# Top-k attention with an ELU feed-forward block: prologue and weight decoding in a written order at two pace levels, exponential and gate for pairs of groups

## The chip, the core and the metric

The kernel runs on one core of a Trainium2 chip. Its engines work side by side, each through a queue of its own: TensorE (PE, matrix products and transposes), VectorE (DVE), ScalarE (ACT), GpSimd (POOL) and SyncE (SP, which here only issues transfers). They wait for each other through semaphores. The metric is the time of one execution in microseconds (us), as the median of several runs.

## The reference

Eight batches of eight heads, 576 tokens, head size 64, all in 32-bit floats. For each row of scores the 32 largest are kept, the others are masked away, and the softmax runs over what is left. The heads of one token are laid side by side (512 numbers), and a feed-forward block follows with an ELU between its products. The two weights come as 64-bit floats.

```python
scores = scale * np.matmul(q, k.transpose(0, 1, 3, 2))
kth = np.partition(scores, -top_k, axis=-1)[..., -top_k:-top_k + 1]
scores = np.where(scores >= kth, scores, -1000000000.0)
attn = np.exp(scores - np.max(scores, axis=-1, keepdims=True))
attn = attn / (np.sum(attn, axis=-1, keepdims=True) + 1e-09)
x = np.matmul(attn, v)          # (B,H,S,D) -> (B*S, H*D)
h = x @ w_in                    # 4608 x 512 by 512 x 2048
g = np.where(h > 0.0, h, np.exp(np.minimum(h, 0.0)) - 1.0)
return g @ w_out                # 2048 x 512
```

## The kernel before

**Attention in steps.** A step is one tile of 128 query rows for one pair of heads; there are 144 of them. For each step PE makes the scores of both heads into PSUM (`scores`, line 291), ScalarE scales them into SBUF (line 308), and VectorE finds the 32nd largest of each row by four maxima of eight and three replacements (lines 319 to 329 in the first eight steps, 341 to 353 later): 14 operations of about 0.74 us. `mask` (lines 366 to 370, GpSimd and ScalarE) turns the row into exponentials, `normalise` (lines 380 to 387, GpSimd) divides, `turn` (line 406) transposes on PE with copies on ScalarE (407), and `attend` (line 432) multiplies by v. Scores are made two steps ahead of the selection; the mask, the transposes and the product with v follow one to three steps behind it.

**Feed-forward in blocks and pieces.** 128, 256 or 384 tokens (a block of one, two or three slots) go through the feed-forward part together, once all their heads are attended (`finish`). Blocks 0 to 4 have one slot, the other fourteen two or three. A block has 16 pieces `hidden(f)`, one for each group of 128 of the 2048 hidden columns, and four pieces `project(s, part)` for each slot. `hidden` makes a product into one of two PSUM buffers (line 490), and three ScalarE operations: n = Relu(-h) (line 502), g = Relu(h) (503), n = exp(-n) (504). VectorE then closes the gate: g + n - 1 (line 471), which is the ELU. A gate isn't issued at once. It goes into the list `gates` with the place at which it was made, and `close_gates(2)` issues it two places later; `project` closes all that are pending, and `hidden` closes the oldest if more than three are. n has five buffers (four for block 0).

**The order of the work.** A planner written in Python issues the pieces between the attention's instructions. Each step has four places, `feed(n, 0.25)`; at each, `feed` works out from the blocks' due times and the pieces' costs (`HIDDEN`, `PROJECT`) how much feed-forward work to issue. From step 8 (`tight`) on the engines take their instructions in just the order in which they are issued (`manual_schedule`). In the steps before it, and in the prologue before those (lines 616 to 633), a scheduler picks by readiness, at compile time.

**The weights' decoding.** The weights are decoded on the chip in 32 pieces of 128 x 512. SP loads one (`load_weight`, 512 KB) into one of three raw buffers; `convert_first` works on its words with three ScalarE operations (lines 169 to 171) and a GpSimd clamp (172), `convert_last` with two VectorE operations (179, 182) and a GpSimd addition into the weight (186). `hook`, called twice in each row's selection in the first eight steps (four times a step) and three times a step later, issues one `decode_piece(i)`: load piece i+2, first half of piece i, last half of piece i-1. A feed-forward piece isn't issued before the weights that it needs are decoded (`decoded`); blocks after the first need all of them. When the last piece is issued, the raw buffers' space goes to the later pools (`late`).

**The prologue** loads k and q of two head pairs and two pieces of weights on SP's queue, transposes k and q (`transpose_qk`, lines 258 to 276), makes the scores of steps 0 and 1, and loads the rest of the first batch.

Of the kernel before, what the change touches and what calls it, by code (L numbers as in the profile page):

```python
# [80 lines left out]
def kernel(  # L81
# [34 lines left out]
    wkpool = pool("wk", 1)  # L116
    etpool = pool("et", 2)
    small = pool("small", 4)
    xtpool = pool("xt", 2)
    opool = pool("o", 1)  # L120
    ps_sc = pool("ps_sc", 1, space=PSUM)
    ps_t = pool("ps_t", 2, space=PSUM)
# [2 lines left out]
    late = {}  # L125
    raws = ExitStack()
    early = raws.enter_context(tc.tile_pool(name="early", bufs=1))
    earlyf = raws.enter_context(tc.tile_pool(name="earlyf", bufs=4))
    rawpool = raws.enter_context(tc.tile_pool(name="raw", bufs=3))

    ident = const.tile([P, P], FP32, tag="ident", name="ident")
    make_identity(nc, ident[:])
# [15 lines left out]
        return moe_w_out[f * P : (f + 1) * P, :], w_out[:, f, :]  # L148

    def load_weight(i):  # L150
        t = rawpool.tile([P, 4 * WN], U32, tag="raw", name="raw")
        nc.sync.dma_start(t[:, 0 : 2 * WN], weight(i)[0])
        raw[i] = t

    def parts(t):
        words = t[:, 0 : 2 * WN].rearrange("p (n w) -> p n w", w=2)
        return words[:, :, 0], words[:, :, 1], t[:, 2 * WN : 3 * WN], t[:, 3 * WN :]

    def convert_first(i):

        lo, hi, e, m = parts(raw[i])
        ef, mf = e.bitcast(FP32), m.bitcast(FP32)
        nc.scalar.activation(ef, hi.bitcast(FP32), AF.Abs, scale=2.0**-48)
        nc.scalar.activation(mf, lo, AF.Copy, scale=2.0**-29, bias=2.0**23)  # L170
        nc.scalar.activation(m.bitcast(I32), mf, AF.Copy, bias=-(2.0**23))
        nc.gpsimd.tensor_scalar(
            ef, ef, (2.0 - 2.0**-3 - 2.0**-23) * 2.0**-32, 2.0**-63, ALU.min, ALU.max
        )

    def convert_last(i):
        t, dst = raw.pop(i), weight(i)[1]
        lo, hi, e, m = parts(t)
        nc.vector.tensor_scalar(
            e, e, 0x0FFFFFFF, 3, ALU.bitwise_and, ALU.logical_shift_left  # L180
        )
        nc.vector.scalar_tensor_tensor(
            out=e, in0=hi, scalar=0x80000000, in1=e,
            op0=ALU.bitwise_and, op1=ALU.bitwise_or,
        )
        nc.gpsimd.tensor_tensor(
            dst.bitcast(I32), e.bitcast(I32), m.bitcast(I32), ALU.add
        )

    decode = []  # L190
# [2 lines left out]
    def hook():  # L193

        if not decode:
            return
        decode.pop(0)()
        if not decode:
            raws.close()
            late["f"] = ctx.enter_context(tc.tile_pool(name="f", bufs=5))  # L200
            late["g"] = ctx.enter_context(tc.tile_pool(name="g", bufs=2))
            late["x"] = ctx.enter_context(tc.tile_pool(name="x", bufs=2))

    def decode_piece(i):
        if i < 2 * NF:
            if i + 2 < 2 * NF:
                load_weight(i + 2)
            convert_first(i)
        if i > 0:
            convert_last(i - 1)  # L210
            decoded[0] = i

    loaded, kqT, vT = {}, {}, {}

    def load_qk(b, hp):

        for name, src in (("k", k), ("q", q)):
            n = J + 1 if name == "k" else J
            t = ldpool.tile([P, n, 2, D], FP32, tag=name + "in", name=name + "in")
            if name == "k":  # L220
                last = t
            for hh in range(2):
                nc.sync.dma_start(
                    t[:, 0:J, hh, :],
                    src[b, 2 * hp + hh, 0:JP, :].rearrange("(p j) d -> p j d", j=J),
                )
            nc.sync.dma_start(
                last[0:R, J, :, :] if name == "k" else last[R:P, J, :, :],
                src[b, 2 * hp : 2 * hp + 2, JP:S, :].rearrange("h p d -> p h d"),
            )  # L230
            loaded[b, hp, name] = t
# [81 lines left out]
    def select_row(u, i):  # L313
        if i == 0:
            u.first = small.tile([P, 2, 8], FP32, tag="m1", name="m1")
            u.last = small.tile([P, 2, 8], FP32, tag="m4", name="m4")
        sc = u.sc[:, i, :]
        m = u.first[:, i, :]
        nc.vector.max(m, sc)
        wk = wkpool.tile([P, S], FP32, tag=f"wk{i}", name="wk")  # L320
        cur = sc
        for r in range(TOP_K // 8 - 1):
            nc.vector.match_replace(wk[:], m, cur, TAKEN)  # L323
            cur = wk[:]
            if r < TOP_K // 8 - 2:
                m = small.tile([P, 8], FP32, tag=f"m{i}", name="m")[:]
            else:
                m = u.last[:, i, :]
            nc.vector.max(m, cur)  # L329
            if r != 1:  # L330
                hook()
                yield

    def select(u):
# [117 lines left out]

    def finish(blk, parts, at, cols, src):
        if blk.xT is None:
            if blk.slots == 1 and late:
                blk.xT = late["x"].tile([P, NC, P], FP32, tag="xT", name="xT")
            else:
                blk.xT = xtpool.tile([P, NC, T], FP32, tag="xT", name="xT")
        nc.scalar.copy(blk.xT[:, at, cols], src)
        blk.left -= parts  # L460
        if blk.left == 0:
            ffn.extend(ffn_pieces(blk))
# [1 line left out]
    gates = []  # L464
    place = [0]

    def close_gates(keep=0):

        while gates and gates[0][0] <= place[0] - keep:
            _, dst, n = gates.pop(0)  # L470
            nc.vector.scalar_tensor_tensor(  # L471
                out=dst, in0=n, scalar=-1.0, in1=dst, op0=ALU.add, op1=ALU.add
            )

    def ffn_pieces(blk):
        n_tok = blk.slots * P

        def hidden(f):
            if f == 0 and blk.number == 0:
                g = early.tile([P, NF, P], FP32, tag="g", name="gT")  # L480
                blk.gT = [g[:, 0:NG], g[:, NG:NF]]
            elif f % NG == 0 and blk.number > 0:
                g = late["g"].tile([P, NG, T], FP32, tag="g", name="gT")
                blk.gT.append(g[:])
            if len(gates) > 3:
                gates[0] = (-1, *gates[0][1:])
                close_gates(place[0])
            ps = ps_f.tile([P, dm], FP32, tag="f", name="hps")
            for i in range(NC):
                nc.tensor.matmul(  # L490
                    ps[:, 0:n_tok],
                    w_in[:, i, f * P : (f + 1) * P],
                    blk.xT[:, i, 0:n_tok],
                    start=(i == 0),
                    stop=(i == NC - 1),
                )
            if blk.number == 0:
                n = earlyf.tile([P, P], FP32, tag="n", name="n")[:]
            else:
                n = late["f"].tile([P, T], FP32, tag="n", name="n")[:, 0:n_tok]  # L500
            g = blk.gT[f // NG][:, f % NG, 0:n_tok]
            nc.scalar.activation(n, ps[:, 0:n_tok], AF.Relu, scale=-1.0)  # L502
            nc.scalar.activation(g, ps[:, 0:n_tok], AF.Relu)  # L503
            nc.scalar.activation(n, n, AF.Exp, scale=-1.0)  # L504
            gates.append((place[0], g, n))

        def project(s, part):
            close_gates()
            if part == 0:
                blk.o = ps_f.tile([P, dm], FP32, tag="f", name="ops")  # L510
            step = NF // 4
            for f in range(part * step, (part + 1) * step):
                nc.tensor.matmul(  # L513
                    blk.o[:],
                    blk.gT[f // NG][:, f % NG, s * P : (s + 1) * P],
                    w_out[:, f, :],
                    start=(f == 0),
                    stop=(f == NF - 1),
                )
# [93 lines left out]
            fed["sum"] += cost  # L613
            piece()

    load_qk(0, 0)
    for i in range(2):
        load_weight(i)
    load_qk(0, 1)
    load_v(0, 0)  # L620
    start_qk(0, 0)
    turn_qk(True)
    scores(steps[0])
    load_qk(0, 2)
    start_qk(0, 1)
    turn_qk(True)
    scores(steps[1])
    load_qk(0, 3)
    for hp in range(1, NHP):
        load_v(0, hp)  # L630
    decode += [lambda i=i: decode_piece(i) for i in range(2 * NF + 1)]
    at(0, start_qk, 0, 2)
    at(1, start_qk, 0, 3)

# [5 lines left out]
    for n in range(NS + 3):  # L640
# [20 lines left out]
                feed(n, 0.25)  # L661
            continue
        if n == tight:
            E = mybir.EngineType
            ctx.enter_context(
                tc.manual_schedule(engines={E.PE, E.Activation, E.DVE, E.Pool})
            )
        passes = select(cur) if cur else iter(range(4))
        if ahead:
            scores(ahead)  # L670
# [59 lines left out]
```

## Time and profile before

| | |
|---|---|
| median of three runs | 1694.66 us (1693.64 to 1695.99) |
| the profiled execution | 1695.23 us, of which the profile's span is 1693.4 us |
| TensorE (PE) | 1597.5 us busy, 94% |
| VectorE (DVE) | 1542.7 us, 91% |
| ScalarE (ACT) | 1179.6 us, 70% |
| GpSimd (POOL) | 627.0 us, 37% |
| granted TensorE clock | 0.974 of full speed in the mean; 0.60 from 40 to 80 us, 0.59 from 80 to 120 us, 1.00 from 160 us on |

The span runs from the first instruction to the last. A row of tenths cuts it into 40 equal slices of 42.3 us, where each digit is an engine's busy share (9 is 90% or more). A line such as "L353 DVE" is the work of line 353 of the kernel on that engine. In a list of waits the name behind the arrow is what ended the wait. An engine that is busy all the time in a stretch sets the time of that stretch; idle time of another costs nothing there.

### The profile page before, as it was taken

The numbers are of one execution on the slowest core, as the hardware profiler recorded it, in microseconds if no ns is written. First come the engines' busy times: TensorE is split into PE (matmuls) and PEld (weight loads), VectorE is DVE, ScalarE is ACT, GpSimd is POOL, SyncE is SP. The second block draws the span as 40 slices with busy tenths as digits, with TensorE's granted clock in tenths as the row PEclk, the third lists the DMA queues.
The fourth block names the chain that finished last, engine by engine and source line by source line (L and its number), as shares of the span: only waits on it lengthen the run. The fifth ranks groups of instructions, "written<-read, shape, count | busy, mean of one in ns | idle before, by whom it ended". The sixth has DMA issues, their size and how long they took to land.

```text
span 1693.4 us, 26805 instructions
## 1 busy us (share of the span) xinstructions
PE 1597.5 (94%) x8560; PEld 1035.0 (61%) x8560; DVE 1542.7 (91%) x3248; ACT 1179.6 (70%) x2813; POOL 627.0 (37%) x1719
## 2 busy tenths in 40 slices
PE   4568899999999999999999999999999999999999
PEld 3355676667575666756557575755557575755565
DVE  6889999999999999999999999999998999998600
ACT  5787776778776776857758585867758686857531
POOL 3675333343333333433333333333333333332200
PEclk8568999999999999999999999999999999999999
DMA  5531021001200111001100111001100000000000
GB/s 156 169 130 63 15 56 36 7 1 42 51 12 7 29 35 42 1 14 42 43 19 1 28 42 35 7 10 46 36 20 8 21 21 28 7 7 7 7 13 13
DMA packets 101131, 56.25 MB, mean 33 GB/s; under 512 B 84096, under 2 KB 92288, under 8 KB 100992
## 3 DMA queue, kind: packets, MB, share of 16 engines
q1 hardware_dynamic: 100992, 54.55, 11.7%
q8 instruction: 68, 1.11, 0.3%
q14 instruction: 71, 0.58, 0.1%
HBM read 45.09 MB, written 9.44 MB: 32 GB/s over the span
## 4 chain that ended last, share of the span: by engine, by line
PE 68%; DVE 21%; ACT 5%; issue 2%; POOL 2%; DMA 1%; SPq 0%; ACTq 0%; POOLq 0%; DVEq 0%
PE ops L513 25%; PE hps L490 21%; PE avps L432 8%; DVE wk L346 7%; PE scps L300 7%; DVE m L353 6%; PE eps L406 5%; DVE m L341 2%; DVE gT L471 1%; DVE wk L323 1%; DVE m L329 1%; PE qkps L270 1%; ACT sc L370 1%; ACT sc L369 1%; ACT et L407 1%
## 5 line engine op out<-in xcount | busy, mean ns | idle before, releaser
L353 DVE MAX8 m<-wk 128x8 f32<-128x576 f32 x816 | 574.9, 745 | 0.0
L490 PE MATMUL hps<-xT,w_in 128*128 128x256 f32 (+2 forms) x2432 | 554.3, 376 | 19.3 <-ACT gT L503 19.3
L513 PE MATMUL ops<-w_out,gT 128*128 128x512 f32 x1152 | 522.6, 598 | 0.0
L490 PEld LDWEIGHTS hps<-xT,w_in 128*128 128x128 f32 x2432 | 409.5, 194 | 119.9 <-ACT gT L503 26.4
L346 DVE MATCH_REPLACE8 wk<-m,wk 128x576 f32<-128x576 f32 x544 | 399.4, 741 | 0.0
L513 PEld LDWEIGHTS ops<-w_out,gT 128*128 128x128 f32 x1152 | 208.4, 190 | 232.8 <-issue 201.0
L380 POOL TENSOR_SCALAR dene<-den 128x2 f32<-128x2 f32 x144 | 34.9, 243 | 819.6 <-ACT sc L370 819.0
L369 ACT ACTIVATE sc<-sc,neg 128x576 f32<-128x576 f32 x288 | 226.5, 787 | 56.6 <-POOL neg L366 56.1
L370 ACT ACTIVATE sc<-sc,gap 128x576 f32<-128x576 f32 x288 | 223.2, 775 | 26.6 <-ACT sc L369 1.9
L308 ACT ACTIVATE sc<-scps 128x576 f32<-128x576 f32 x288 | 173.4, 661 | 82.4 <-PE scps L300 82.4
L387 POOL TENSOR_SCALAR sc<-sc,rec 128x576 f32<-128x576 f32 x288 | 218.7, 769 | 15.2 <-POOL rec L385 0.4
L300 PE MATMUL scps<-kqT 64*128 64x288 f32 (+1 forms) x1280 | 198.1, 438 | 21.5 <-ACT sc L308 14.7
L471 DVE SCALAR_TENSOR_TENSOR gT<-n,gT 128x256 f32<-128x256 f32 (+2 forms) x304 | 129.1, 431 | 95.3 <-ACT n L504 95.3
L407 ACT COPY et<-eps 128x512 f32<-128x512 f32 x288 | 167.4, 581 | 61.8 <-PE eps L406 61.8
L406 PEld LDWEIGHTS eps<-ident,sc 128*128 128x128 f32 x1152 | 144.5, 145 | 93.4 <-issue 48.9
L346 DVE MATCH_REPLACE8 wk<-m,sc 128x576 f32<-128x576 f32 x272 | 199.7, 741 | 0.0
L432 PE MATMUL avps<-et,vT 128*64 128x256 f32 (+2 forms) x2080 | 191.0, 325 | 9.0 <-ACT et L407 8.4
L406 PE MATMUL eps<-ident,sc 128*128 128x128 f32 x1152 | 177.9, 280 | 21.8 <-POOL sc L387 18.6
L341 DVE MAX8 m<-sc 128x8 f32<-128x576 f32 x272 | 191.3, 744 | 0.0
L432 PEld LDWEIGHTS avps<-et,vT 128*64 128x64 f32 x2080 | 122.3, 140 | 80.4 <-issue 24.7
L502 ACT ACTIVATE n<-hps 128x256 f32<-128x256 f32 (+2 forms) x304 | 112.6, 370 | 84.2 <-PE hps L490 79.0
L300 PEld LDWEIGHTS scps<-kqT 64*128 64x128 f32 (+1 forms) x1280 | 106.0, 180 | 90.2 <-issue 45.1
(47 smaller groups left out, 1236.6 us busy)
## 6 DMA issues: line engine op xcount, KB each, us to landing
kin<-in_k_dram SPq DMA_DIRECT2D x64, 128.0 KB, 2.8
qin<-in_q_dram SPq DMA_DIRECT2D x64, 128.0 KB, 2.8
raw<-in_moe_w_in_dram SPq DMA_DIRECT2D x16, 512.0 KB, 3.9
vT<-in_v_dram SPq DMA_DIRECT2D x64, 128.0 KB, 2.3
raw<-in_moe_w_out_dram SPq DMA_DIRECT2D x16, 512.0 KB, 3.3
out_dram<-osb SPq DMA_DIRECT2D x32, 256.0 KB, 2.2
kin<-in_k_dram SPq DMA_DIRECT2D x32, 32.0 KB, 2.5
kin<-in_q_dram SPq DMA_DIRECT2D x32, 32.0 KB, 2.2
```

The source lines that it names most:

```text
L300: nc.tensor.matmul(wide[i][rows, half, 0:HS], kq[part, q0 : q0 + u.t.ql], kq[part, k0 : k0 + HS], start=True, stop=True,)
L341: nc.vector.max(found[i], cur[i])
L346: nc.vector.match_replace(wk[i], found[i], cur[i], TAKEN)
L353: nc.vector.max(found[i], cur[i])
L369: nc.scalar.activation(sc, sc, AF.Prelu, bias=neg[:], alpha=STEEP)
L370: nc.scalar.activation(sc, sc, AF.Exp, bias=gap[:], accum_out=u.den[:, i : i + 1])
L387: nc.gpsimd.tensor_scalar(u.sc[:, i, :], u.sc[:, i, :], rec[:, i : i + 1], 1.0, ALU.mult, ALU.mult)
L406: nc.tensor.transpose(ps[:, c * P : (c + 1) * P], sc[:, c0 : c0 + P], ident[:])
L407: nc.scalar.copy(g.et[:, chunks, u.at, :], ps[:, 0 : n * P].rearrange("p (c q) -> p c q", c=n),)
L432: nc.tensor.matmul(ps[i * D : (i + 1) * D, cols], vt[:, 2 * J + i if c == J else i * J + c, :], w, start=(c == 0), stop=(c == J),)
L490: nc.tensor.matmul(ps[:, 0:n_tok], w_in[:, i, f * P : (f + 1) * P], blk.xT[:, i, 0:n_tok], start=(i == 0), stop=(i == NC - 1),)
L513: nc.tensor.matmul(blk.o[:], blk.gT[f // NG][:, f % NG, s * P : (s + 1) * P], w_out[:, f, :], start=(f == 0), stop=(f == NF - 1),)
```

## The change

Five things change together.

- **Prologue.** The engines' order is written out (`manual_schedule`) for the transposes and scores of steps 0 and 1. `load_qk(0, 0)` sends its three q transfers through ScalarE's queue, and the second weight piece is loaded behind k and q of the second head pair.
- **Decoding.** In steps 0 to 3 (query tile 0) `hook` is called once in each row (two a step), in steps 4 to 7 three times in each row (six a step). The last half of a piece follows two hooks behind its first half, not one, so that there are 34 hooks. A raw buffer is 3 x 512 words, not 4 x 512, since the low part is converted in place, and there are five, not three.
- **Exponential and gate in pairs.** n holds two groups. The two Relu operations of each group stay as they are; after the odd group one exponential runs over both, and one gate closes both. There are two such buffers. An even group first closes the oldest pair if more than one is pending.
- **Gates before a projection.** `project(s, part)` closes the pending gates only up to the last group that it reads.
- **Pools.** xT of blocks of one slot has three buffers of that size; larger blocks take theirs from the space that the decoding leaves.

```diff
-    earlyf = raws.enter_context(tc.tile_pool(name="earlyf", bufs=4))
-    rawpool = raws.enter_context(tc.tile_pool(name="raw", bufs=3))
+    earlyf = raws.enter_context(tc.tile_pool(name="earlyf", bufs=2))
+    rawpool = raws.enter_context(tc.tile_pool(name="raw", bufs=5))
...
-        lo, hi, e, m = parts(raw[i])
-        ef, mf = e.bitcast(FP32), m.bitcast(FP32)
+        lo, hi, e = parts(raw[i])
+        ef, mf = e.bitcast(FP32), lo.bitcast(FP32)
         nc.scalar.activation(ef, hi.bitcast(FP32), AF.Abs, scale=2.0**-48)
         nc.scalar.activation(mf, lo, AF.Copy, scale=2.0**-29, bias=2.0**23)
-        nc.scalar.activation(m.bitcast(I32), mf, AF.Copy, bias=-(2.0**23))
+        nc.scalar.activation(lo.bitcast(I32), mf, AF.Copy, bias=-(2.0**23))
...
-            late["f"] = ctx.enter_context(tc.tile_pool(name="f", bufs=5))
+            late["f"] = ctx.enter_context(tc.tile_pool(name="f", bufs=2))
...
-        if i > 0:
-            convert_last(i - 1)
-            decoded[0] = i
+        if i > 1:
+            convert_last(i - 2)
+            decoded[0] = i - 1
...
-    def load_qk(b, hp):
+    def load_qk(b, hp, other=nc.sync):
...
-            n = J + 1 if name == "k" else J
+            n, queue = (J + 1, nc.sync) if name == "k" else (J, other)
...
             nc.vector.max(m, cur)
+            if r == 2 or u.t.qt > 0:
+                hook()
             if r != 1:
-                hook()
                 yield
...
-    def close_gates(keep=0):
-
-        while gates and gates[0][0] <= place[0] - keep:
-            _, dst, n = gates.pop(0)
+    def close_gates(keep=0, upto=None):
+        while gates:
+            put, group, dst, n = gates[0]
+            if put > place[0] - keep if upto is None else group > upto:
+                return
+            gates.pop(0)
...
-            if len(gates) > 3:
-                gates[0] = (-1, *gates[0][1:])
-                close_gates(place[0])
+            if f % 2 == 0:
+                if len(gates) > 1:
+                    close_gates(upto=gates[0][1])
+                if blk.number == 0:
+                    n = earlyf.tile([P, 2, P], FP32, tag="n", name="n")
+                else:
+                    n = late["f"].tile([P, 2, T], FP32, tag="n", name="n")
+                blk.n = n[:, :, 0:n_tok]
...
-            nc.scalar.activation(n, ps[:, 0:n_tok], AF.Relu, scale=-1.0)
-            nc.scalar.activation(g, ps[:, 0:n_tok], AF.Relu)
-            nc.scalar.activation(n, n, AF.Exp, scale=-1.0)
-            gates.append((place[0], g, n))
+            g = blk.gT[f // NG]
+            nc.scalar.activation(blk.n[:, f % 2, :], ps[:, 0:n_tok], AF.Relu, scale=-1.0)
+            nc.scalar.activation(g[:, f % NG, 0:n_tok], ps[:, 0:n_tok], AF.Relu)
+            if f % 2 == 1:
+                nc.scalar.activation(blk.n, blk.n, AF.Exp, scale=-1.0)
+                dst = g[:, f % NG - 1 : f % NG + 1, 0:n_tok]
+                gates.append((place[0], (blk.number, f - 1), dst, blk.n))
 
         def project(s, part):
-            close_gates()
+            close_gates(upto=(blk.number, (part + 1) * NF // 4 - 1))
...
-    load_qk(0, 0)
-    for i in range(2):
-        load_weight(i)
+    load_qk(0, 0, nc.scalar)
+    load_weight(0)
     load_qk(0, 1)
+    load_weight(1)
     load_v(0, 0)
-    start_qk(0, 0)
-    turn_qk(True)
-    scores(steps[0])
+    with tc.manual_schedule(engines=engines):
+        for hp in range(2):
+            start_qk(0, hp)
+            turn_qk(True)
+            scores(steps[hp])
     load_qk(0, 2)
-    start_qk(0, 1)
-    turn_qk(True)
-    scores(steps[1])
     load_qk(0, 3)
```

More of the change, by code (lines that the diff above doesn't have):

```diff
@@ L118 @@
     small = pool("small", 4)
-    xtpool = pool("xt", 2)
+    xpool = pool("x", 3)
     opool = pool("o", 1)
@@ L150, in load_weight @@
     def load_weight(i):
-        t = rawpool.tile([P, 4 * WN], U32, tag="raw", name="raw")
+        t = rawpool.tile([P, 3 * WN], U32, tag="raw", name="raw")
         nc.sync.dma_start(t[:, 0 : 2 * WN], weight(i)[0])
@@ L156, in parts @@
         words = t[:, 0 : 2 * WN].rearrange("p (n w) -> p n w", w=2)
-        return words[:, :, 0], words[:, :, 1], t[:, 2 * WN : 3 * WN], t[:, 3 * WN :]
+        return words[:, :, 0], words[:, :, 1], t[:, 2 * WN :]
     def convert_first(i):
-        lo, hi, e, m = parts(raw[i])
-        ef, mf = e.bitcast(FP32), m.bitcast(FP32)
+        lo, hi, e = parts(raw[i])
+        ef, mf = e.bitcast(FP32), lo.bitcast(FP32)
         nc.scalar.activation(ef, hi.bitcast(FP32), AF.Abs, scale=2.0**-48)
         nc.scalar.activation(mf, lo, AF.Copy, scale=2.0**-29, bias=2.0**23)
-        nc.scalar.activation(m.bitcast(I32), mf, AF.Copy, bias=-(2.0**23))
+        nc.scalar.activation(lo.bitcast(I32), mf, AF.Copy, bias=-(2.0**23))
         nc.gpsimd.tensor_scalar(
@@ L177, in convert_last @@
         t, dst = raw.pop(i), weight(i)[1]
-        lo, hi, e, m = parts(t)
+        lo, hi, e = parts(t)
         nc.vector.tensor_scalar(
@@ L186, in convert_last @@
         nc.gpsimd.tensor_tensor(
-            dst.bitcast(I32), e.bitcast(I32), m.bitcast(I32), ALU.add
+            dst.bitcast(I32), e.bitcast(I32), lo.bitcast(I32), ALU.add
         )
@@ L199, in hook @@
             raws.close()
-            late["f"] = ctx.enter_context(tc.tile_pool(name="f", bufs=5))
+            late["f"] = ctx.enter_context(tc.tile_pool(name="f", bufs=2))
             late["g"] = ctx.enter_context(tc.tile_pool(name="g", bufs=2))
-            late["x"] = ctx.enter_context(tc.tile_pool(name="x", bufs=2))
+            late["x"] = ctx.enter_context(tc.tile_pool(name="xt", bufs=2))
     def decode_piece(i):
@@ L222, in load_qk @@
             for hh in range(2):
-                nc.sync.dma_start(
+                queue.dma_start(
                     t[:, 0:J, hh, :],
@@ L226, in load_qk @@
                 )
-            nc.sync.dma_start(
+            queue.dma_start(
                 last[0:R, J, :, :] if name == "k" else last[R:P, J, :, :],
@@ L454, in finish @@
         if blk.xT is None:
-            if blk.slots == 1 and late:
-                blk.xT = late["x"].tile([P, NC, P], FP32, tag="xT", name="xT")
+            if blk.slots == 1:
+                blk.xT = xpool.tile([P, NC, P], FP32, tag="xT", name="xT")
             else:
-                blk.xT = xtpool.tile([P, NC, T], FP32, tag="xT", name="xT")
+                blk.xT = late["x"].tile([P, NC, T], FP32, tag="xT", name="xT")
         nc.scalar.copy(blk.xT[:, at, cols], src)
@@ L496, in hidden @@
                 )
[L497 to L502, printed above, removed]
-            nc.scalar.activation(g, ps[:, 0:n_tok], AF.Relu)
-            nc.scalar.activation(n, n, AF.Exp, scale=-1.0)
-            gates.append((place[0], g, n))
+            g = blk.gT[f // NG]
[5 more added lines that the diff above has]
+                gates.append((place[0], (blk.number, f - 1), dst, blk.n))
         def project(s, part):
-            close_gates()
+            close_gates(upto=(blk.number, (part + 1) * NF // 4 - 1))
             if part == 0:
@@ L614, in feed @@
             piece()
-    load_qk(0, 0)
-    for i in range(2):
-        load_weight(i)
+    E = mybir.EngineType
+    engines = {E.PE, E.Activation, E.DVE, E.Pool}
+    load_qk(0, 0, nc.scalar)
+    load_weight(0)
     load_qk(0, 1)
+    load_weight(1)
     load_v(0, 0)
-    start_qk(0, 0)
-    turn_qk(True)
-    scores(steps[0])
+    with tc.manual_schedule(engines=engines):
[3 more added lines that the diff above has]
+            scores(steps[hp])
     load_qk(0, 2)
-    start_qk(0, 1)
-    turn_qk(True)
-    scores(steps[1])
     load_qk(0, 3)
@@ L630 @@
         load_v(0, hp)
-    decode += [lambda i=i: decode_piece(i) for i in range(2 * NF + 1)]
+    decode += [lambda i=i: decode_piece(i) for i in range(2 * NF + 2)]
     at(0, start_qk, 0, 2)
@@ L663 @@
         if n == tight:
[L664 to L667, printed above, removed]
+            ctx.enter_context(tc.manual_schedule(engines=engines))
         passes = select(cur) if cur else iter(range(4))
```

## The prediction

> **What bounds the kernel now.** I read the busy tenths first, then cut the span into stretches at the places where they change, then asked each engine what it waited for in the first stretches, and last read the first microseconds instruction by instruction. The busy tenths:
>
> ```profile
> PE   4568899999999999999999999999999999999999
> DVE  6889999999999999999999999999998999998600
> ACT  5787776778776776857758585867758686857531
> ```
>
> PE (TensorE) is full from the sixth slice to the end, VectorE from the fourth until two slices before the end; ScalarE (ACT) is nowhere full. The stretches, with columns for start:end, length, busy time of PE, weight loads, VectorE, ScalarE and GpSimd (instruction counts in brackets), granted clock, DMA share and GB/s:
>
> ```profile
> 0.00:16.00 16.00, 5.85 (x23) 4.25 (x24) 3.41 (x5) 6.12 (x11) 3.92 (x14) 1.00 0.68 167
> 16.00:80.00 64.00, 33.39 (x151) 22.26 (x150) 56.83 (x104) 44.84 (x89) 36.96 (x65) 0.67 0.57 160
> 80.00:150.30 70.30, 49.80 (x266) 38.63 (x265) 64.10 (x125) 57.87 (x143) 49.79 (x77) 0.69 0.39 128
> 150.30:200.00 49.70, 44.63 (x312) 31.82 (x309) 49.67 (x111) 35.02 (x103) 19.14 (x49) 1.00 0.02 7
> 200.00:300.00 100.00, 92.42 (x747) 66.09 (x746) 100.00 (x221) 74.41 (x209) 37.15 (x113) 1.00 0.17 42
> 300.00:600.00 300.00, 288.39 (x1602) 194.54 (x1601) 300.00 (x648) 224.33 (x553) 113.17 (x333) 1.00 0.09 22
> 600.00:1600.00 1000.00, 993.57 (x5166) 624.76 (x5166) 961.92 (x2025) 712.82 (x1645) 362.81 (x1059) 1.00 0.08 22
> ```
>
> The cuts are the first selection on VectorE (about 16 us), the start of step 4 (80) and of step 8 (150.3, the first maximum of line 341). Three regimes follow. Before 150.3 VectorE leads but stands idle for 12.6 + 7.2 + 6.2 = 26.0 us. From 150.3 to 600 it is never idle, and PE has 5.1 + 7.6 + 11.6 = 24.3 us to spare. From 600 PE is 99.4% busy, and VectorE has the slack. So the end is set by VectorE up to 600 and by PE after it: a microsecond taken from VectorE before 600 moves everything behind it, up to PE's 24.3 us of slack after 150.3 (what is won before 150.3 costs PE nothing, for it is idle there for 61 us). After 600 less work on VectorE or ScalarE is worth nothing.
>
> What VectorE and ScalarE wait for in the decoding (waiting line, releaser, total us, times, longest):
>
> ```profile
> DVE raw L179 <- POOL raw L172: 25.2, 12, 11.2
> ...
> ACT raw L169 <- DMA raw<-in_moe_w_in_dram: 14.4, 8, 7.8
> ```
>
> Nearly all of the 26.0 us is one wait: the decoding's first VectorE operation on GpSimd's clamp. 11.2 us of it is the start. There ScalarE takes the weights before the attention:
>
> ```profile
> 9.85 0.66 ACT L169 ACTIVATE raw<-raw 128x512 f32<-128x512 f32 x1 [7.85 <-DMA raw<-in_moe_w_in_dram]
> 10.41 0.30 ACT L263 COPY kqT<-scps 128x192 f32<-128x192 f32 x1
> ...
> 15.91 1.42 DVE L319 MAX8 m<-sc 128x8 f32<-128x576 f32 x2
> ```
>
> It sits in front of the weight's transfer until 9.85, although PE's last transpose for it ended at 9.14 and the first at 7.43; the first selection starts at 15.91.
>
> **The start of selection.** PE's first matmul waits for q until 6.77. The three q transfers (1.28 + 0.63 us of issue on SP, from 2.82) go to ScalarE's queue and start beside k's at about 0.7. ScalarE has nothing else to do until 9.85, so its 1.9 us of issue and its table load (1.28) lie under that idle time; SP sends weight piece 0 some 2 us earlier. Weight piece 1 is issued behind the six transfers of the second head pair (4.2 us of issue), v behind it; neither is read before the first pass. I take 1.3 us off PE's start. The manual order then puts the two kqT copies ahead of any decoding: PE ends at 7.8, the last copy takes to 8.4, scores 2.3 us, sc 0.7, so VectorE could start at 11.4; with semaphore hand-over 11.8. Ends: 11.0 and 13.0 (q lands no earlier, since the transfers share the DMA engines at a share of 0.68).
>
> **Steps 0 to 3.** VectorE was busy 56.8 us of 64. The decoding costs it 0.681 + 0.746 = 1.43 us a piece (means of lines 179 and 182). Of the 32 pieces 2 were closed before 16 us, 11 between 16 and 80, 17 between 80 and 150.3, 2 after. At one hook a row, with the closing half two hooks behind, steps 0 to 3 close 6 and steps 4 to 7 close 24, leaving again 2. So here 56.8 - 5 x 1.43 = 49.7. Of the idle 7.2 us I keep 2.5: a piece's clamp now has two hooks' time before VectorE reads it, and with five slots a load waits for the piece three before it, not for the one just before it. Together 52.2 us.
>
> **Steps 4 to 7.** VectorE: 64.1 + 7 x 1.43 = 74.1. Block 0's gates cost less. Fourteen of them (line 471) ran here with a median of 0.698 us where one alone takes 0.27:
>
> ```profile
> 129.01 0.28 DVE L471 SCALAR_TENSOR_TENSOR gT<-n,gT 128x128 f32<-128x128 f32 x1
> ...
> 130.55 0.91 DVE L471 SCALAR_TENSOR_TENSOR gT<-n,gT 128x128 f32<-128x128 f32 x1
> ```
>
> Eight double ones at 0.77 (0.64, the mean over 10.3 us in 16, and 0.13 for the added columns) in place of 10.3 us save 4 us: 70.1. [...] By mean durations alone the seven added pieces cost their 10.0 us and no more. [...] I take 1.6. Idle: of 6.2 us I keep 4.5, more than above, because ScalarE becomes nearly full. Its part of a piece is three operations 0.55 us apart (12.14, 12.69, 13.21 in the trace), 1.65 us; 57.9 + 8 x 1.65 = 71.1 us. GpSimd has 65 us. DMA: 24 pieces of 0.5 MB in 76 us are 165 GB/s, as between 16 and 80 (160 at a share of 0.57), so it has room. Together 70.1 + 1.6 + 4.5 = 76.2.
>
> Step 8 starts at 11.8 + 52.2 + 76.2 = 140.2, not 150.3: **10.1 us** won. With no idle time left and no added collision: 11.0 + 49.7 + 70.1 = 130.8, 19.5 us won.
>
> **Exponential and gate for two groups.** A gate's start to the next instruction is 0.19, 0.33 and 0.46 us at 128, 256 and 384 columns, so 0.06 is the fixed part. Between 160 and 600 there are 104 gates, 52 pairs: 3.1 us off VectorE, on the path. The other pairs save VectorE time after 600, under PE. On ScalarE the exponential's spacing is 0.20, 0.30, 0.41 at these widths: 0.095 fixed, 152 x 0.095 = 14.4 us in all. [...]
>
> **The gates' wait.** Closing only what a projection reads changes little. By the planner's costs and due times all FFN pieces fall where they fell, and before a projection forced only 4 of the 289 gates ahead of their age of two places; block 0's projections start in step 8 either way. What the pair adds is a wait. n had five slots of one group and now has two of a pair: the Relu of group f (even) must wait for the gate of groups f-4 and f-3, which falls two places (half a step) after group f-3. Behind a waiting Relu in ScalarE's queue stand the sc and et copies and masks; PE's next product waits for the PSUM slot. I took, from the trace, each even Relu's start less the end of the gate of group f-3. In block 1 group 4 starts at 179.97 and that gate ends at 184.30: 4.3 us late. In blocks 1 to 4 seventeen are late or have under 0.3 us to spare, in block 6 three are late by up to 1.9, in block 8 two; after 710 none is late, and the median is 5 us early. Once ScalarE has been pulled back by 4.3 us the next ones (3.0, 3.1, 2.4) are on time. VectorE does not wait for this, and it is the bound there. But PE loses its lead of some 3 us, and between 284 and 310 VectorE's gates lag the exponentials by only 3.0 to 4.6; there VectorE would wait about 1. With the 1.7 of block 8, where PE is the bound: 2 us lost. Ends: 0, and 29 if each late one costs in full.
>
> **Sum.** 10.1 + 3.1 - 2.0 = 11.2 us. The profiled execution took 1695.23 us, its span was 1693.4, so 1.8 lies around it; the median of the three runs is 1694.66. The span becomes 1682.2, the median **1683.5 us**. The tail from 1600 (last block's FFN on PE alone, 27.6 + 27.5 us in the chain) stays.
>
> **Rivals.** *ScalarE becomes the bound of steps 4 to 7.* It needs 71.1 us; if it keeps the 12.4 us that it was idle in 80 to 150.3, those steps take 83.5, step 8 starts at 11.8 + 52.2 + 83.5 = 147.5, 2.8 won, and with the gates 3.9: 1690.8. For it: 71 of 76 us; against: it was idle waiting for data that now come earlier. Between it and the first case lie 1686 to 1690.
> *Nothing reaches the end*: the scheduler fills the first eight steps by readiness, so it may place the later decoding where VectorE then waits as long as now, and the early start goes into that wait; 1692 to 1697.
> *The pair's slots lock ScalarE to VectorE* (slower). Place: the Relu of every even group in blocks 1 to 8, 170 to 710 us. If the Relu's delay makes the next exponential and so the next gate late, VectorE waits too, and the delays add rather than absorb. The late starts sum to 29 us: 1694.7 - 13.2 + 29 = 1710. From 13 us of it the change is slower than no change. For it: PE is 92 to 96% busy there, so what it loses is hard to regain, and ScalarE already waited for the gate:
>
> ```profile
> ACT n L502 <- DVE gT L471: 2.3, 2, 1.5
> ```
>
> Against: VectorE is behind ScalarE in just these places, and gates are two places old.
>
> **Chances.** First case 0.52 (own range 1675 to 1688), ScalarE 0.20, nothing 0.08, slots 0.20. A measurement of this kernel tells about 0.2% (3.4 us) from no change. Nearly all of the first two are faster by more than that: 0.72; same 0.08; slower 0.20. The range: below, 1694.7 - 19.5 - 3.1 = 1672; above, it takes in the smaller half of the slots' case, 1700.
>
> **What would show it.** The first maximum at about 12 us with no decoding before it; step 8 at about 140; line 179's wait at 5 to 8 us in all after the first; ScalarE over 90% busy in steps 4 to 7; Relus (n from hps) waiting for gates by some 4 to 10 us in all between 160 and 360; PE idle between 150 and 600 about 20 us. Wrong would be: VectorE idle over 20 us before step 8, or VectorE waiting for exponentials before 600 by more than 5 us.

## The result, and the profile after

The changed kernel takes 1682.9 us (median of four runs, 1682.55 to 1683.16) against 1694.57 for the kernel before beside it: 11.7 us less, a ratio of 0.9931 with a 95% interval of 0.9918 to 0.9944. The forecast was 1683.5. The number was met, but not by the sum that led to it: of its terms the first failed, the next two were off in opposite directions, and that of the pairs was too small.

The busy tenths of the changed kernel:

```profile
PE   6767999999999999999999999999999999999999
DVE  6999999999999999999999999999998999998600
ACT  6776786778776776767768685857758586857531
```

VectorE is full from the second slice on, where before it had two eights. The stretches of the changed kernel, with the columns as before (16, 80, 200, 300 and 600 are cuts of before, 139.8 is about where step 8 was forecast to begin):

```profile
0.00:16.00 16.00, 5.77 (x23) 4.30 (x24) 2.52 (x5) 7.01 (x13) 3.81 (x14) 1.00 0.77 188
16.00:80.00 64.00, 51.24 (x210) 33.62 (x210) 64.00 (x124) 49.91 (x100) 38.48 (x72) 0.62 0.53 155
80.00:139.80 59.80, 40.01 (x205) 32.59 (x203) 54.08 (x88) 48.37 (x117) 46.63 (x66) 0.66 0.43 145
...
200.00:300.00 100.00, 93.26 (x784) 68.01 (x783) 98.57 (x210) 73.17 (x192) 36.56 (x112) 1.00 0.17 42
300.00:600.00 300.00, 290.83 (x1595) 195.80 (x1595) 299.34 (x619) 225.63 (x533) 116.91 (x335) 1.00 0.09 24
```

Between 16 and 80 us VectorE is busy 64.00 of 64 us, where it was 56.83. All its idle time there is gone; between 80 and 139.8 it is still idle for 5.7. The start looks as it did. First instructions of the changed kernel:

```profile
8.34 0.66 ACT L170 ACTIVATE raw<-raw 128x512 f32<-128x512 f32 x1 [4.29 <-DMA raw<-in_moe_w_in_dram]
...
10.15 0.31 ACT L264 COPY kqT<-scps 128x192 f32<-128x192 f32 x1
...
15.64 1.42 DVE L320 MAX8 m<-sc 128x8 f32<-128x576 f32 x2
```

ScalarE still waits for weight piece 0 and decodes it ahead of the kqT copies, and the first selection starts at 15.64 us, not at the 11.8 of the forecast.

Where the time comes from is best read from two clocks: when VectorE begins a step, and when ScalarE copies out a finished output tile, which PE has then completed. From the timelines, us (difference to before in brackets):

| | before | after | pairs left out | pairs alone | decoding alone | prologue alone |
|---|---|---|---|---|---|---|
| VectorE, step 4 | 79.7 | 58.0 | 58.0 | 79.4 | 60.6 | 79.3 |
| VectorE, step 8 | 150.3 | 146.5 (-3.8) | 146.1 | 151.6 | 150.3 | 154.3 |
| VectorE, step 10 | 174.1 | 168.2 (-5.8) | 168.4 (-5.7) | 175.4 (+1.3) | 172.5 (-1.6) | 175.0 (+0.9) |
| VectorE, step 68 | 772.5 | 762.3 (-10.2) | 769.8 (-2.6) | 769.8 (-2.6) | 773.9 (+1.4) | 773.9 (+1.4) |
| PE, 1st output tile | 168.6 | 167.0 (-1.6) | 168.0 (-0.6) | 172.6 (+4.0) | 171.1 (+2.5) | 169.8 (+1.2) |
| PE, 2nd | 223.6 | 219.9 (-3.8) | 220.8 (-2.8) | 227.1 (+3.5) | 224.0 (+0.3) | 224.5 (+0.9) |
| PE, 7th | 477.1 | 472.0 (-5.2) | 474.3 (-2.8) | 479.5 (+2.4) | 479.0 (+1.9) | 477.9 (+0.8) |
| PE, 11th | 663.4 | 655.6 (-7.8) | 661.8 (-1.6) | 663.2 (-0.2) | 664.8 (+1.4) | 665.9 (+2.5) |
| PE, 12th | 734.9 | 723.6 (-11.3) | 730.4 (-4.5) | 731.2 (-3.7) | 736.2 (+1.2) | 734.5 (-0.4) |
| PE, 36th (last) | 1689.6 | 1676.9 (-12.7) | 1684.7 (-4.9) | 1684.5 (-5.1) | 1690.5 (+0.9) | 1688.8 (-0.8) |

The last four columns are the experiments below. Step 8 is counted from the first maximum in the fixed order. In the kernel before that one was placed ahead of the last maximum of step 7, which starts at 151.99 us. Counted from there VectorE wins 5.5 us by step 8, which fits the 5.8 at step 10. Two things stand out in the second column. VectorE wins 5.8 us by step 10, but PE only 3.8 by its second tile. And between the 7th and the 12th tile PE wins another 6.1, where the forecast had almost nothing.

### The profile page after: what moved, and what is told of

Same layout as the page of the kernel before. It is cut to its first block, busy times and chain, and to the rows that moved or that the text cites. A ratio compares the mean times of both kernels' runs of the same rounds, so it can differ in the third digit from the quotient of the medians.

```text
span 1680.8 us, 26396 instructions
## 1 busy us (share of the span) xinstructions
PE 1604.5 (95%) x8560; PEld 1041.7 (62%) x8560; DVE 1534.4 (91%) x3096; ACT 1167.5 (69%) x2661; POOL 638.8 (38%) x1719
## 4 chain that ended last, share of the span: by engine, by line
PE 59%; DVE 26%; ACT 5%; issue 1%; POOL 1%; ACTq 0%; DVEq 0%; POOLq 0%
PE ops L523 22%; PE hps L502 19%; DVE wk L348 11%; DVE m L355 9%; PE avps L434 7%; PE scps L301 6%; PE eps L408 4%; DVE m L343 3%; DVE gT L478 2%; ACT sc L372 1%; ACT sc L371 1%; PE qkps L271 1%; ACT et L409 1%; PE scps L408 1%; ACT n L510 0%
## 5 line engine op out<-in xcount | busy, mean ns | idle before, releaser
L478 DVE SCALAR_TENSOR_TENSOR gT<-n,gT 128x512 f32<-128x512 f32 (+2 forms) x152 | 106.5, 701 | 97.7 <-ACT n L513 97.6
```

## The experiments

Two theories were put against each other once the result was known. **A**: the prologue is worth nothing, the decoding about 5.8 us, and the pairs of gates the rest, on VectorE, which is the bound until some 735 us. **B**: the prediction's own sum, 10.1 us from prologue and decoding and 1.1 net from the pairs. The four kernels ran beside the same runs of the kernel before (median 1694.23). Some causes below are read from traces and were not tried; the text says where.

### The prologue alone

```diff
 # the kernel before, with
+    load_qk(0, 0, nc.scalar)
+    load_weight(0)
     load_qk(0, 1)
+    load_weight(1)
     load_v(0, 0)
+    with tc.manual_schedule(engines=engines):
+        for hp in range(2):
+            start_qk(0, hp)
+            turn_qk(True)
+            scores(steps[hp])
```

> The kernel before with the prologue alone (written order for steps 0 and 1, q on ScalarE's queue, weight piece 1 later). Theory A: within 1 us of before, first selection at 15.5 to 16 us. Theory B: 4 us faster, first selection at 12 us.

Measured: 1694.55 us, ratio 1.0001 (0.9992 to 1.0011). A holds: nothing was won, and the first selection is at 15.68. The prologue's instructions on ScalarE, PE and VectorE:

```profile
8.58 0.66 ACT L169 ACTIVATE raw<-raw 128x512 f32<-128x512 f32 x1 [4.54 <-DMA raw<-in_moe_w_in_dram]
...
10.36 0.30 ACT L263 COPY kqT<-scps 128x192 f32<-128x192 f32 x1
...
11.69 2.29 PE L300 MATMUL scps<-kqT 64*128 64x288 f32 x8 [3.50 <-ACT kqT L276]
...
13.13 0.67 ACT L169 ACTIVATE raw<-raw 128x512 f32<-128x512 f32 x1 [1.50 <-DMA raw<-in_moe_w_in_dram]
...
14.25 1.17 ACT L308 ACTIVATE sc<-scps 128x576 f32<-128x576 f32 x2
14.60 0.43 DVE L179 TENSOR_SCALAR raw<-raw 128x512 uint32<-128x512 uint32 x1 [3.48 <-POOL raw L172]
...
15.06 0.69 DVE L182 SCALAR_TENSOR_TENSOR raw<-raw 128x512 uint32<-128x512 uint32 x1
...
15.68 1.41 DVE L319 MAX8 m<-sc 128x8 f32<-128x576 f32 x2
```

In this trace the instructions inside the written order keep it, but those issued later are placed among them. The decoding of piece 0, which belongs to the steps behind it, still goes first on ScalarE (8.58 us; the first kqT copy 10.36). PE's first matmul starts 0.95 us earlier than before (5.82 us; 6.77), the first kqT copy only 0.05 (10.36; 10.41). The written order does win something on PE: the scores of step 0 start 1.2 us earlier (11.69; 12.90). In the kernel before a transpose of the second head pair stood ahead of them and waited for its k:

```profile
12.52 0.45 PE L270 MATMUL qkps<-ident,kin 128*128 128x128 f32 x1 [3.38 <-DMA kin<-in_k_dram]
...
12.90 2.29 PE L300 MATMUL scps<-kqT 64*128 64x288 f32 x8
```

But weight piece 1 then does what piece 0 did. ScalarE begins with it at 13.13 and scales the scores behind it (14.25), and on VectorE its two operations stand ahead of the first maximum. At the first selection 0.2 us is left (15.68; 15.91). The changed kernel shows the same: scores at 11.48, scaled from 14.21 on, piece 1 on VectorE from 14.57 to 15.72, the first maximum at 15.64.

### The decoding alone

```diff
 # the kernel before, with
-    rawpool = raws.enter_context(tc.tile_pool(name="raw", bufs=3))
+    rawpool = raws.enter_context(tc.tile_pool(name="raw", bufs=5))
...
+            if r == 2 or u.t.qt > 0:
+                hook()
...
-        if i > 0:
-            convert_last(i - 1)
-            decoded[0] = i
+        if i > 1:
+            convert_last(i - 2)
+            decoded[0] = i - 1
 # and the low part converted in place, and xT's pools as changed
```

> The kernel before with the decoding of the changed one (two paces, last half two hooks behind, five raw buffers of 3 x 512 words, xT's pools moved to make room), prologue and gates as before. Theory A (the prologue is worth nothing, since ScalarE still decodes piece 0 ahead of the kqT copies): 5 to 6 us faster than before, as fast as the kernel with prologue and decoding within 1 us. Theory B: 6 us faster, and 4 us slower than with the prologue.

Measured: 1695.98 us, ratio 1.0007 (0.9998 to 1.0017). Both theories were wrong: the decoding alone wins nothing. It does what it was to do on VectorE in part (step 4 at 60.6 us in place of 79.7, step 10 at -1.6 us), but PE is 2.5 us late at its first tile. The wait is in PE's timeline at the place where the eps transposes of step 7 are due:

```profile
164.42 1.12 PE L408 MATMUL eps<-ident,sc 128*128 128x128 f32 x4 [6.08 <-POOL sc L389]
```

The kernel before has no such wait there. The changed kernel has it too, and its trace shows what GpSimd does in the meantime:

```profile
151.30 3.70 PE L523 MATMUL ops<-w_out,gT 128*128 128x512 f32 x8
160.16 1.12 PE L408 MATMUL eps<-ident,sc 128*128 128x128 f32 x4 [5.15 <-POOL sc L389]
```

```profile
156.02 1.28 POOL L187 TENSOR_TENSOR w_out<-raw 128x512 int32<-128x512 int32 x1 [2.54 <-issue]
157.39 0.23 POOL L382 TENSOR_SCALAR dene<-den 128x2 f32<-128x2 f32 x1
...
159.35 1.47 POOL L389 TENSOR_SCALAR sc<-sc,rec 128x576 f32<-128x576 f32 x2
```

With the last half two hooks behind, the decoding has 34 hooks and not 33, and the last falls in the second pass of step 8. From step 8 on the order is fixed: on GpSimd the normalisation of step 7 stands behind the last piece's addition (line 187), which waits for VectorE's part (155.19 to 155.88). PE stands still from 155.0 to 160.2, and its granted clock falls as well; the four transposes at 160.16 take 1.12 us, where the same four take 0.60 before (at 163.91). The stretches (columns as above, the clock being third from the end):

```profile
155.00:160.00 5.00, 0.00 (x1) 0.00 (x0) 4.96 (x12) 0.00 (x0) 3.46 (x7) 0.78 0.00 0
160.00:165.00 5.00, 4.84 (x13) 3.18 (x14) 5.00 (x11) 3.75 (x9) 1.51 (x6) 0.54 0.00 0
165.00:170.00 5.00, 5.00 (x39) 3.04 (x38) 5.00 (x11) 2.59 (x6) 3.69 (x11) 1.00 0.15 54
```

The kernel before has the same order on GpSimd, with the last piece's addition ahead of the normalisation:

```profile
159.11 1.27 POOL L186 TENSOR_TENSOR w_out<-raw 128x512 int32<-128x512 int32 x1 [3.51 <-DVE raw L182]
```

There the normalisation ends at 163.90, later than in the changed kernel, and the eps transposes start at 163.91. But PE is busy with products and scores until then (5.00 us in each five from 150 to 165), while in the changed kernel it has none left at 155.0. So the gap takes two things: a normalisation that stands behind the decoding, and a PE for which nothing else was issued ahead of the transposes.

All three kernels with the new decoding have the gap (5.15, 6.07 and 6.08 us). The three without it have no gap over 2.12 us after 145; they wait for the same GpSimd line at 139 to 141 (2.58, 3.65 and 1.65 us), in the steps that the scheduler orders. In the three with the gap PE's second tile falls behind VectorE's win at step 10, by 2.0, 2.9 and 1.9 us. But pairs alone, without it, falls behind by 2.2 too (and prologue alone by 0), so these differences don't single it out. A kernel that closes the last pieces before step 8 was not tried: what the gap costs in the end, and how much of it the 34th hook makes, stays open.

### Prologue and decoding, without pairs

```diff
 # the changed kernel, with
-            if f % 2 == 1:
-                nc.scalar.activation(blk.n, blk.n, AF.Exp, scale=-1.0)
-                dst = g[:, f % NG - 1 : f % NG + 1, 0:n_tok]
-                gates.append((place[0], (blk.number, f - 1), dst, blk.n))
+            nc.scalar.activation(n, n, AF.Exp, scale=-1.0)
+            gates.append((place[0], g, n))
 # n with five buffers of one group, gates closed as before
```

> Prologue and decoding as in the changed kernel; exponential, gates and n buffers as before. The changed kernel is 11.7 us faster than before; its step 8 begins 3.8 us earlier, step 10 5.8 us. Theory A (now held: decoding gives about 5.8 us up to step 10, pairs of gates the rest on VectorE, which is the bound until some 735 us and not 600): 5 to 6.5 us faster than before, so 5 to 7 us slower than the changed kernel. Theory B (the prediction's own sum: 10.1 from prologue and decoding, 1.1 net from the pairs): 10 us faster than before.

Measured: 1690.7 us, ratio 0.9980 (0.9970 to 0.9989): 3.5 us faster than before. That is below both theories, well below B. So prologue and decoding, 0.3 and 1.8 us slower alone (neither clear of noise), win 3.5 together. VectorE's win does not last: 5.7 us at step 10, 2.6 at step 68. Between the two steps it waits for exponentials for 2.2 us, where the kernel before does not wait at all. The two kernels with the decoding differ in VectorE's waits between 16 and 80 us: here it is busy 64.00 of 64, there 60.04, with this wait in the list:

```profile
DVE raw L180 <- POOL raw L173: 4.0, 2, 2.1
```

With the written prologue the order of the next eight steps comes out differently, and better, as the pair of runs shows. That the compile-time scheduler starts from another state there is the author's guess; why the order comes out better wasn't traced further.

### Pairs alone

```diff
 # the kernel before, with
-            nc.scalar.activation(n, n, AF.Exp, scale=-1.0)
-            gates.append((place[0], g, n))
+            if f % 2 == 1:
+                nc.scalar.activation(blk.n, blk.n, AF.Exp, scale=-1.0)
+                dst = g[:, f % NG - 1 : f % NG + 1, 0:n_tok]
+                gates.append((place[0], (blk.number, f - 1), dst, blk.n))
...
-            close_gates()
+            close_gates(upto=(blk.number, (part + 1) * NF // 4 - 1))
 # n with two buffers of a pair
```

> The kernel before with the exponential and the gate for pairs and the gates closed as far as read, nothing else. Theory A: 5.5 to 7 us faster than before. Theory B (3.1 us won on VectorE, 2 lost to the slots): 1 us faster. If the pair's slots lock ScalarE to VectorE it would be slower than before.

Measured: 1690.16 us, ratio 0.9974 (0.9964 to 0.9984): 4.1 us faster, between the theories, and no lock of ScalarE to VectorE. The table says why it is not more: 4.0 us are lost on PE by its first tile, in the steps that the scheduler orders and at their end, and 9.1 are won after it (from +4.0 to -5.1). In the changed kernel the first tile comes 1.0 us earlier than without the pairs, not later. So the loss belongs to how the first eight steps come out with the old prologue and decoding, and not to the pairs' steady work. It would also explain why the parts don't add: 3.5 and 4.1 make 7.6, together they make 11.7. That gates are closed only as far as a projection reads came with the pairs in this run; the two were not separated.

**Where the pairs' gain lies.** For the most part from the 7th to the 12th tile: there the two kernels with pairs win 6.1 us, the three other changed ones 0.7 to 1.7. The kernel before has two gaps on PE there, of 1.39 us each, before the scores. The first, on PE and on ScalarE:

```profile
537.53 0.75 PE L300 MATMUL scps<-kqT 64*128 64x288 f32 x2
539.67 1.23 PE L300 MATMUL scps<-kqT 64*128 64x288 f32 x6 [1.39 <-ACT et L407]
```

```profile
537.25 0.78 ACT L369 ACTIVATE sc<-sc,neg 128x576 f32<-128x576 f32 x1 [3.04 <-POOL neg L366]
538.12 0.77 ACT L370 ACTIVATE sc<-sc,gap 128x576 f32<-128x576 f32 x1
...
539.35 0.27 ACT L407 COPY et<-scps 128x128 f32<-128x128 f32 x1
```

PE waits for a PSUM area that ScalarE has to copy out; the copy stands behind the mask; the mask has waited 3.04 us for GpSimd's negation, and that for VectorE's last maximum of the row (the first of the two from 536.15 to 537.56). So VectorE is late, and in this stretch it is the bound: it is busy 255.00 of the 255 us from 480 to 735. Before, the mask begins 0.35 us ahead of the end of PE's transposes (537.25; 537.60). In the changed kernel it begins 2.7 us ahead (529.39; 532.05), and the scores follow the transposes at once:

```profile
531.98 1.60 PE L301 MATMUL scps<-kqT 64*128 64x288 f32 x8
```

The second gap, at 723.7 us, costs more than itself, since the granted clock falls behind it. The kernel before:

```profile
720.00:725.00 5.00, 3.70 (x16) 1.91 (x14) 5.00 (x13) 2.25 (x6) 0.74 (x4) 1.00 0.01 3
725.00:730.00 5.00, 4.62 (x22) 2.51 (x24) 5.00 (x13) 3.14 (x7) 2.81 (x7) 0.73 0.00 0
730.00:735.00 5.00, 5.00 (x17) 2.27 (x14) 5.00 (x11) 0.46 (x2) 0.93 (x5) 0.93 0.00 0
```

5 us at 0.73 and 5 at 0.93 are 1.7 us of clock (an estimate from these rows), on top of the 1.39. The changed kernel wins 3.5 between the 11th and the 12th tile. That place alone does not show the pairs' worth, since the prologue alone and the kernel without pairs win 2.9 there as well: they have their gap and their drop of the clock at the first place, and lose 1.7 and 1.2 us between the 7th and the 11th tile. The two places have to be taken together. The four kernels without pairs have a gap of 1.15 to 1.40 us at one of them or at both, and a drop of the clock behind one (0.73, 0.85, 0.83 and 0.77 in the first stretch of five): behind the second where there are two, else behind the only one. The two kernels with pairs have neither gap there. One execution of each was profiled, so whether the drop would come at the same place again isn't known. Whether it is VectorE's time or ScalarE's that pays was not separated by a run of its own (one exponential for a pair with two gates, or the reverse). The chain of waits speaks for VectorE.

## Why the prediction came out right, and where its steps failed

- **The start (4.1 us): failed.** The step rests on the sentence that the manual order puts the kqT copies ahead of any decoding. It doesn't, neither for piece 0 on ScalarE nor for piece 1 on ScalarE and VectorE; 0.3 us was measured, and the prologue alone is worth nothing. Nor does a run show the 0.4 us that it added for hand-overs by semaphore: in the changed kernel the scores begin 0.04 us after the end of the last kqT copy (11.44; 11.48).
- **Steps 0 to 3 (52.2 us): 42.4 measured**, from 15.64 to 58.05. VectorE's idle time there is 0, not 2.5. Of the six pieces two are closed before the first selection, as before; the sum had counted them after it, since it had the selection start at 11.8. And the four that are left cost 1.10 us each (0.426 + 0.676), where 1.43 had been taken and the kernel before pays 1.66 in these steps.
- **Steps 4 to 7 (76.2 us): 88.4 measured**, to 146.48. Idle time was about right (5.7 us, forecast 4.5). VectorE's busy time was not: 82.7 us, forecast 71.7. The term that was too small is the collision with GpSimd, taken at 1.6 us. The two VectorE operations of the decoding, in the kernel before (80 to 150.3 us) and in the changed one (58 to 146.5 us):

```profile
L182 DVE SCALAR_TENSOR_TENSOR raw<-raw 128x512 uint32<-128x512 uint32 x17 | 12.8, 750 | 0.0
...
L179 DVE TENSOR_SCALAR raw<-raw 128x512 uint32<-128x512 uint32 x16 | 8.2, 515 | 5.6 <-POOL raw L172 5.6
```

```profile
L183 DVE SCALAR_TENSOR_TENSOR raw<-raw 128x512 uint32<-128x512 uint32 x24 | 21.9, 911 | 0.0
L180 DVE TENSOR_SCALAR raw<-raw 128x512 uint32<-128x512 uint32 x24 | 20.8, 865 | 5.7 <-POOL raw L173 5.7
```

By the prediction's terms the 24 pieces should have taken 33.1 us (17 at 1.27, seven more at 1.43, 1.6 of collision); they took 42.7. In the timeline 21 of the 48 operations overlap with an addition of GpSimd (line 187), with a mean of 1.17 us for line 180 and 1.44 for line 183; the other 27 have 0.44 and 0.69. Before, 6 of 33 overlap with one in steps 4 to 7. In steps 0 to 3 it is the other way round: 10 of 23 before, 1 of 8 now. These overlaps do not follow GpSimd's busy share: it was 57% in steps 0 to 3 and 71% in steps 4 to 7 before, and 50 and 76% now. (The 65 us that the prediction gave GpSimd in steps 4 to 7, 49.8 before and about 1.9 for each of eight added pieces, were near the 67.5 measured.) The longest forms here (1.52 and 1.78 us) exceed the short ones (0.40 and 0.67) by about 1.1, with an addition taking 1.3; before, line 179 took from 0.40 to 1.49. That is read from the traces; no run took the additions away. The 1.6 us of the forecast are shown by no run: they were the author's estimate. Without them the 24 pieces come to 31.5 us, so 11.2 were measured in their place. The prediction had also taken the means over the whole trace (0.681 and 0.746), which mix stretches with many and with few collisions; over the whole trace they rose to 0.754 and 0.854. ScalarE's time was forecast well (71.1 us, measured 71.5), but in 88.4 us it did not become the bound.
- **The sum up to step 8: 10.1 us forecast, 3.8 measured** (5.5 by the count of maxima), 5.8 by step 10, and only 3.8 on PE at its second tile. What is won on VectorE before step 8 is not free for PE: behind the step "what is won before 150.3 costs PE nothing" PE stands still for 5.15 us at the normalisation of step 7. The prediction had counted the hooks, and had not followed GpSimd's queue in step 8.
- **The pairs on VectorE (3.1 us): the unit was right, the region too short.** In the median a gate takes 0.191, 0.324 and 0.590 us at 128, 256 and 512 columns up to the next instruction, so a pair saves 0.06. From step 10 to step 68 VectorE wins 4.4 us more (5.8 to 10.2). The gates take 31.9 us there in place of 38.0. Of these 6.1 us the fixed part of 65 pairs is 3.9, and the rest comes from fewer gates that run longer than the median. Of what is won, 2.1 us go to waits (next point). The prediction let VectorE's rule end at 600, because it read one window of 1000 us behind that (961.92 busy); cut finer, VectorE is full up to 800 (135.00 us of 135 and 65.00 of 65 in the kernel before). And on PE the win is larger than the 4.4, with the two gaps and the drop of the clock gone. What the pairs save on ScalarE has no term in the sum, since ScalarE was nowhere full (busy for 74.4 us of 100 from 200 us on, and for 224.3 of the next 300, in the kernel before): its exponentials went from 125.3 us of busy time to 93.7 (lines 504 and 513), and no run separates their worth.
- **The slots (2 us lost): the wait is there, its cause is not clear.** ScalarE waited for gates for 6.1 us in all (five times; 3.6 between 160 and 360, forecast 4 to 10). VectorE waits for exponentials for 2.1 us between steps 10 and 68 in the changed kernel and for 2.4 with the pairs alone, where the kernel before does not wait. But the two kernels that have the new decoding and no pairs wait for 2.2 and 2.0, with five buffers of one group. So against the kernel before the wait has the forecast size, and beside the new decoding the pairs add nothing to it. It is contained in the 4.4 us, and a third buffer wasn't tried.

```profile
ACT n L510 <- DVE gT L478: 6.1, 5, 1.7
```

The same list for VectorE, from step 10 to step 68:

```profile
DVE gT L478 <- ACT n L513: 2.1, 2, 1.4
```

- **The rivals.** ScalarE as the bound and the slots' lock did not come. "Nothing reaches the end" gives the time of prologue or decoding taken alone, but not for its reason: with the decoding alone VectorE is idle for 20.2 us before step 8, not as long as before (26.0).
- **The signs.** None came as stated: the first maximum at 15.64 us (forecast about 12), step 8 at 146.5 (about 140), the wait for the clamp 9.4 us after the first (5 to 8), ScalarE 81% busy in steps 4 to 7 (over 90), Relus waiting for gates 3.6 us (4 to 10), PE idle for 24.5 us between 150 and 600 (about 20). Of the two signs of being wrong, VectorE's idle time before step 8 missed its mark of 20 us by 0.8 (19.2: 13.5 in the start, none in steps 0 to 3, 5.7 after).

So two misses cancelled, and that the number was met is luck. The sum put nearly all of its 11.2 us before 480 us, where PE's seventh tile shows 5.2; behind it, where the sum had at most 1 left, PE won 7.5. The direction rested on a sound reading (VectorE idle for 26 us before step 8, and the bound after it).

## What to carry to other kernels

An order that is written out for a part of a program did not keep later work out of that part here (the decoding began at 8.34 us on ScalarE, the kqT copies at 10.15); look at the queue of the engine that matters before a gain is counted on it. When a pipeline gets one stage longer, follow its last pieces through every queue to the point where the order becomes fixed: here an addition on GpSimd stood in front of the normalisation that PE needed next, and PE stood still for 5.15 us. Take the price of an operation from the stretch in which it will run, and not from the whole trace: the same two operations cost 1.10 us a piece in one stretch and 1.78 in the next. And cut the windows where the bound changes; one long window from 600 us on hid 200 us in which VectorE was still full.

## What the runs showed of the hardware that was not expected

The granted clock of TensorE fell after gaps of 1.2 to 1.6 us in otherwise full stretches: to between 0.73 and 0.85 in one stretch of 5 us and 0.81 to 0.93 in the next. It seldom did. Between 170 and 1680 us PE has 14 gaps of 1.0 to 1.65 us in the kernel before and nine in the changed one; the clock fell (below 0.97 in a stretch of 5 us) behind one of the 14 and none of the nine. In the six traces it fell five times there (once before, once without pairs, twice with the decoding alone, once with the prologue alone, never in the two kernels with pairs); what sets these five apart was not found. The gap of 5 to 6 us ahead of step 7's transposes was followed by a stretch of 5 us at 0.54 in the changed kernel, 0.50 without the pairs and 0.64 with the decoding alone. So one small stall of PE, of 1.39 us, cost about twice its length (with the 1.7 us of clock estimated above), but behind most of those counted no fall shows.

VectorE's two decoding operations took 0.40 to 0.43 us and 0.67 to 0.69 where GpSimd did nothing in the meantime, and up to 1.52 and 1.78 beside its additions of 1.3 us, in the changed kernel. No run took the additions away, so that these are the cause is read from the overlaps alone.
